# Three products of 12-bit parts in one Fourier stage, and a new order for two quarters, in a fused Fourier mixing and long-convolution kernel

## The chip, the core and the metric

The kernel runs on one core of one Trainium2 chip. The metric is the device time of one execution in microseconds (us); for a program on one core that is the time of that core. The core's engines work in parallel, each through its own list of instructions in fixed order: TensorE (PE, matmuls; PEld in the profile are its weight loads), VectorE (DVE), ScalarE (ACT), GpSimd (POOL) and SyncE (SP), which in this kernel issues nearly all DMA transfers. Engines wait for each other through semaphores. SBUF is the on-chip memory, PSUM the small memory that matmuls write to, in banks of 512 columns of 32-bit numbers.

## What is computed

Two heads that share nothing, put side by side. Head A is Fourier mixing of x (2048 x 512) by four given DFT matrices; head B is a long convolution of u with a kernel K that is made from state-space parameters.

```python
# A
a = einsum("bsd,ed->bse", x, dft_hid_re)
b = einsum("bsd,ed->bse", x, dft_hid_im)
y = einsum("ts,bse->bte", dft_seq_re, a) - einsum("ts,bse->bte", dft_seq_im, b)
# B
dt = exp(log_dt)
A = -exp(log_A_real) + 1j * A_imag
C = (C_real + 1j * C_imag) * dt[:, None]
P = exp((A * dt[:, None])[:, :, None] * pos[None, None, :])     # pos = 0..2047
K = 2.0 * einsum("dn,dnl->dl", C, P).real                       # 512 x 2048 taps
Kf, Uf = rfft(K, 4096), rfft(u.transpose(0, 2, 1), 4096)
y = irfft(Uf * Kf[None], 4096)[:, :, :2048].transpose(0, 2, 1) + u * D_skip
```

The results are 32-bit; inputs and outputs are too.

## The kernel before

**Head A (class `Fnet`), the stream.** All of A is 128 x 128 by 128 x 512 matmuls in 12 groups of four PSUM accumulators: eight groups over 16 tiles of x and the sequence matrices, whose results go to DRAM (`p`), then four groups over 8 tiles each of the hidden matrices and `p`. A 32-bit factor is cut in two parts, `hi` (a copy on ACT to the type `F32R`, which keeps 12 bits of the fraction, L184) and `lo` (the rest, a subtraction on DVE to the same type, L188). Each product is then three matmuls of one pass, hi·hi, hi·lo and lo·hi (L304): 1,920 in all. During the first group the raw tiles of x lie in a buffer named `uk` that is borrowed from head B (`loads`, L231) until all 16 are split.

**Head B (class `Ssm`).** The taps of K are sums of powers, made on DVE and ACT from tables (`tables1`, `tables2`, lines L543 to L684) in 16 chunks of 32 channels. For each chunk `taps` multiplies two tables on PE (L739, 128 small passes). Two chunks make one `stage1_k` (L769, eight in all): the first stage of the kernel's Fourier transform, its copies out of PSUM on ACT (L778) and a store to DRAM (`xk`, L783). `spectrum_u` and `stage1_u` do the same for u in eight calls: load (L808), four full-precision matmuls of 64 rows by 512 columns (L814; the chip runs each as two passes), copies on ACT (L824), store (`xu`, L830). The channels then go in four quarters h of 128, each in four groups q:

- `spectra` and `load_spectrum` load a group's part of `xu` and `xk` (L867), quarter by quarter, when all of that quarter's `xk` is stored (`xk_ev`);
- `products` and `product`: the second Fourier stage of u and k (L894, 64 passes), two copies on ACT (L906), six DVE operations for the complex product (L909 to L922), then the first stage of the inverse (`run`, L929, 32 passes), two copies on ACT (L944), a store to `zs` (L950);
- `inverses` and `inverse`: when all four groups of a quarter are stored, two loads from `zs` (L970), the last stage (L975, 32 passes), copies (L981) and the store of the result (L984).

The inverse's first stage has a way to join the taps: while taps are still to come (`taps_left`), a product hands its `run` to a list (`waiting`), and the next call of `taps` runs it right ahead of its own matmuls, in the same visit to PE and the same pair of PSUM slots. There are two such slots, of two banks each (`banks`, `give`), for all of head B.

**Buffers.** Head B has two sets of buffers. Set 0 has one buffer each of `xt`, `uk`, `z` and `zl` and is there from the start; set 1 has two of each and gets its memory only when the tables' memory is given back, after the last kernel's store (`tab_ev`). Quarters 0 to 2 use set 0, quarter 3 uses set 1 (`h // 3`).

**The order.** All instructions are put in order ahead of time, in Python, by a planner (class `Plan`). Each piece of work is a generator that names an engine and a duration before each instruction; the planner always takes the piece that can start first, and among equals the one of lower urgency number. It charges extra when PE changes between the stream and other work. The stream's matmuls have urgency 5, all other PE work less, so the stream fills what head B leaves. The stream's splits have urgency 0 (3 when three are ahead); u's stage has 1, tables 2 and more.

Of the kernel before, what the change touches and what calls it, by code (L numbers as in the profile page):

```python
# [365 lines left out]
class Ssm:  # L366


    def __init__(self, tc, ctx, plan, nd, ldt, dsk, uG, f1u, f1k, w2, ia, ib, out):
        self.tc, self.nc, self.plan = tc, tc.nc, plan  # L370
        self.nd, self.ldt, self.uG, self.out = nd, ldt, uG, out
        self.const = ctx.enter_context(tc.tile_pool(name="b_const", bufs=1))
        self.fps = ctx.enter_context(tc.tile_pool(name="b_fps", bufs=1, space=PSUM))
        dram = ctx.enter_context(tc.tile_pool(name="b_dram", bufs=1, space=DRAM))
        self.xu = dram.tile([64, 2, 32, DM], F32, name="xu")
        self.xk, self.zs = (dram.tile([4, 64, 2, 32, PART], F32, name=n) for n in ("xk", "zs"))
        self.dt_dram = dram.tile([128, 4], F32, name="dt_dram")
        self.par_dram = dram.tile([128, 4, DM - FIRST], F32, name="par_dram")
        first = ("f1u", f1u), ("f1k", f1k), ("dskip", dsk)
        second = ("w2", w2), ("ia", ia), ("ib", ib)  # L380
        self.cst = [[(n, self.const.tile([128, *a.shape[1:]], F32, name=n), a) for n, a in s] for s in (first, second)]
        self.halfpi = self.const.tile([128, 1], F32, name="halfpi")
        self.slots, self.fs, self.one = [0, 1], Sem(2), Sem(1)
        self.t1s, self.t2s, self.css = Sem(2), Sem(1), Sem(2)
        self.kss, self.res, self.xks = Sem(1), Sem(1), Sem(1)
        self.waiting, self.taps_left, self.pars = [], 16, Sem(1)
        self.sets, self.set_ev = {}, [Event(), Event()]
        self.const_ev, self.const2_ev, self.xu_ev = Event(), Event(), Event()
        self.xk_ev, self.zs_ev = [Event() for _ in range(4)], [Event() for _ in range(4)]

    def set_buffers(self, i, pool):
        self.sets[i] = Buffers(pool, i + 1)
# [12 lines left out]
    def constants(self, which, ev):  # L405
        yield "dma", sum(load(4 * math.prod(a.shape) / 1024) for _, _, a in self.cst[which])
        for n, t, a in self.cst[which]:
            self.nc.sync.dma_start(t, a)
            setattr(self, n, t)
        if ev is self.const_ev:  # L410
            yield "dve", 0.3
            self.nc.vector.tensor_scalar(self.dskip, self.dskip, 0.5, None, op0=OP.mult)
        self.plan.set(ev)

    def banks(self, n):

        yield self.one
        got = []
        for _ in range(n):
            yield self.fs  # L420
            k = self.slots.pop(0)
            got.append((k, self.fps.tile([128, 2, 512], F32, name=f"f{k}")))
        self.plan.put(self.one)
        return got

    def give(self, k):
        self.slots.append(k)
# [329 lines left out]
    def stage1_k(self, ks, n, ev):  # L757

        nc = self.nc
        yield ev  # L760
        yield "pool", 0.2
        nc.gpsimd.tensor_tensor(ks[:, :, 0], self.dskip[:, 16 * n:16 * n + 16], ks[:, :, 0], op=OP.add)
        yield self.const_ev
        got = yield from self.banks(2)
        yield "pe", 1.82
        for a in range(2):
            for j in range(4):
                r = slice(32 * j, 32 * j + 32)
                nc.tensor.matmul(got[j // 2][1][:, j % 2], self.f1k[r, a], ks[r, :, 32 * a:32 * a + 32],  # L769
                                 start=a == 0, stop=a == 1, tile_position=(32 * j, 0))  # L770
        self.plan.put(self.kss)
        yield self.xks
        xs = self.tab.tile([128, 32, 64], F32, name="xk_sb")
        for h, (k, p) in enumerate(got):
            for j in range(2):
                yield "act", act(512)
                o = 32 * h + 16 * j
                nc.scalar.activation(xs[:, :, o:o + 16], p[:, j].rearrange("p (i l) -> p l i", i=16), AF.Copy)  # L778
            self.give(k)
        xk = self.xk[n // 2].rearrange("s c l d -> (s c) l d")[:, :, 64 * (n % 2):64 * (n % 2) + 64]  # L780
        yield "dma", load(1024)
        for k in range(4):
            nc.sync.dma_start(xk[:, 8 * k:8 * k + 8], xs[:, 8 * k:8 * k + 8])  # L783
        self.plan.put(self.xks)
        if n % 2:
            self.plan.set(self.xk_ev[n // 2])
        if n == 7:
            self.plan.set(self.tab_ev)

    def spectrum_u(self):  # L790

        self.uleft = 16
        yield self.const_ev
        b = self.sets[0]
        yield b.zls
        self.xu_sb, self.xus = b.pool.tile([128, 2, 2, DM], F32, name="zl", bufs=b.n), Sem(2)
        for k in range(8):
            name = "uk"[k % 2]
            yield b.xts[name]
            if not k:  # L800
                self.u_sb = b.pool.tile([128, 2, 2, DM], F32, name="xt", bufs=b.n)
            self.plan.spawn(self.stage1_u(k, name), 1)

    def stage1_u(self, k, name):
        nc, b = self.nc, self.sets[0]
        u = self.u_sb[:, k % 2]
        yield "dma", load(512)
        nc.sync.dma_start(u, self.uG[:, 2 * k:2 * k + 2])  # L808
        got = yield from self.banks(2)
        yield "pe", 1.82  # L810
        for m in range(2):
            for r in range(2):
                rows = slice(64 * r, 64 * r + 64)
                nc.tensor.matmul(got[m][1][:, r], self.f1u[rows], u[rows, m], start=True, stop=True,  # L814
                                 tile_position=(64 * r, 0))
        self.plan.put(b.xts[name])
        for m in range(2):
            n = 2 * k + m
            sem = b.zbs if n % 3 == 2 else self.xus
            yield sem  # L820
            x = b.pool.tile([128, 2, DM], F32, name="z", bufs=b.n) if n % 3 == 2 else self.xu_sb[:, n % 3]
            for r in range(2):
                yield "act", act(512)
                nc.scalar.activation(x[:, r], got[m][1][:, r], AF.Copy)  # L824
            self.give(got[m][0])
            self.plan.spawn(self.store_u(x, 2 * k + m, sem), 1)

    def store_u(self, x, m, sem):
        yield "dma", load(512)
        self.nc.sync.dma_start(self.xu.rearrange("s c l d -> (s c) l d")[:, 2 * m:2 * m + 2], x)  # L830
        self.plan.put(sem)
        self.uleft -= 1
        if not self.uleft:
            self.plan.put(self.sets[0].zls)
            self.plan.set(self.xu_ev)

    def quarters(self):


        self.plan.spawn(self.constants(1, self.const2_ev), 3)  # L840
        self.left, self.xt = [4] * 4, {}
        self.xt_ev = {(n, h, q): Event() for n in "uk" for h in range(4) for q in range(4)}
        xu = [self.xu[:, :, :, PART * h:PART * h + PART] for h in range(4)]
        self.plan.spawn(self.spectra("u", xu, [self.xu_ev] * 4), 1)
        self.plan.spawn(self.spectra("k", [self.xk[h] for h in range(4)], self.xk_ev), 1)
        self.plan.spawn(self.products(), 1)
        for h in range(4):
            self.plan.spawn(self.inverses(h), 1)

    def spectra(self, name, x, evs):  # L850
        yield self.const2_ev
        for h in range(4):
            yield evs[h]
            yield self.set_ev[h // 3]
            b = self.sets[h // 3]
            view = x[h].rearrange("(q x g) c l d -> q (g c l) x d", q=8, x=4)
            for q in range(4):
                yield b.xts[name]
                self.plan.spawn(self.load_spectrum(b, name, h, q, view), 1)

    def load_spectrum(self, b, name, h, q, view):
        if (h, q) not in self.xt:
# [6 lines left out]

    def products(self):  # L870
        for h in range(4):
            yield self.set_ev[h // 3]
            b = self.sets[h // 3]
            for q in range(4):
                for n in "uk":
                    yield self.xt_ev[n, h, q]
                yield b.uks
# [5 lines left out]
    def product(self, b, h, q, got, done):  # L883
# [45 lines left out]
                        nc.tensor.matmul(got[xx // 2][1][64 * g:64 * g + 64, xx % 2, :2 * PART], self.ia[rows, c],  # L929
                                         Y[rows, :, g, 0], start=c == 0, stop=c == 1, tile_position=(32 * xx, 64 * g))  # L930
        w = Joined(self, run)
        if self.taps_left:
            self.waiting.append(w)
            yield w
        if w.got is None:
# [4 lines left out]
        yield b.zbs  # L940
        z = b.pool.tile([128, 2, 4, PART], F32, name="z", bufs=b.n)
        for n, (k, p) in enumerate(w.got):
            yield "act", act(512)
            a.activation(z[:, :, 2 * n:2 * n + 2].rearrange("p r x d -> p x r d"),  # L944
                         p[:, :, :2 * PART].rearrange("p x (r d) -> p x r d", r=2), AF.Copy)
            w.leave(k)
        view = self.zs[h].rearrange("(q x g) c l d -> q (g c l) x d", q=8, x=4)
        yield "dma", load(512)
# [114 lines left out]
```

## Time and profile before

| | us |
|---|---|
| three runs | 588.68, 590.52, 588.62 |
| median | 588.68 |
| the profiled execution | 590.22 |
| its span, first to last instruction | 588.4 |

| lines | what | instructions on PE |
|---|---|---|
| L304 | stream | 1,920 |
| L739 | taps | 2,048 |
| L769 | kernel, first Fourier stage | 128 |
| L814 | u, first Fourier stage | 64 |
| L894 | second Fourier stage | 1,024 |
| L929 | inverse, first stage | 512 |
| L975 | inverse, last stage | 256 |

How to read the profile: its second part cuts the span in 40 slices (14.7 us each here) and gives the busy share of each engine in tenths. PEclk is the granted clock of PE in tenths of full speed. A group's row has the line, the engine, the operation, output <- inputs by the program's names, the shapes and the count, then busy time, the mean ns of one, and the idle time of the engine just before, with what ended it. A matmul's recorded duration includes its way through the array and overlaps the next one, so the pace of matmuls is read from their starts. The chain of waits lists start, length and what ran, back from the last instruction. In the view of waits, a row has the total, the count and the longest wait. SPq and ACTq are the issues of transfers.

### The profile page before, as it was taken

Reading aid. Unit: us, or ns where it says so; the run is one execution under the profiler, and the core shown is the slowest. Engines: PE = TensorE matmul, PEld = TensorE weight load, DVE = VectorE, ACT = ScalarE, POOL = GpSimd, SP = SyncE. Lnnn points to the kernel's source line nnn. Section 1 sums busy time; section 2 is a strip of 40 time slices with the busy share of each in tenths; the row PEclk is TensorE's granted clock in tenths of the full one; section 3 lists DMA queues with packets and bytes.
Section 4 is the critical chain, followed back from the end, with each engine's and each line's share of the span. In section 5 each row is a group of like instructions: output and inputs, shape, how many; then the busy total and the mean of one; then the engine's idle time right before and its main releaser. Section 6 shows DMA issues by size and latency. Waiting matters only on the chain.

```text
span 588.4 us, 14902 instructions
## 1 busy us (share of the span) xinstructions
PE 580.2 (99%) x5958; PEld 439.7 (75%) x5958; DVE 496.5 (84%) x883; ACT 380.8 (65%) x745; POOL 4.7 (1%) x12
## 2 busy tenths in 40 slices
PE   8999999999999999999999999999999999999997
PEld 6767668778778777877687778777877776876785
DVE  7986989999999999999999999999999954245420
ACT  4789884946676677758674876577764635264622
POOL 0000000000000000000000000000000000000000
PEclk9999999999999999999999999999999999999999
DMA  8999996363493369446768684559798744998674
GB/s 262 329 367 338 337 342 199 101 188 81 122 280 106 89 170 264 137 135 165 246 183 259 168 246 128 136 158 284 225 282 234 230 131 148 283 354 263 190 251 144
DMA packets 141238, 125.84 MB, mean 214 GB/s; under 512 B 46192, under 2 KB 106352, under 8 KB 140912
## 3 DMA queue, kind: packets, MB, share of 16 engines
q1 hardware_dynamic: 140880, 124.48, 69.4%
q8 instruction: 47, 0.77, 0.5%
q10 hardware_dynamic: 288, 0.39, 0.2%
q14 instruction: 23, 0.19, 0.1%
HBM read 82.12 MB, written 42.73 MB: 212 GB/s over the span
## 4 chain that ended last, share of the span: by engine, by line
PE 69%; DVE 21%; issue 4%; DMA 3%; ACT 2%; SPq 1%; DVEq 0%; ACTq 0%
PE acc L304 52%; DVE prod L543 7%; DVE lo L188 4%; DVE t L552 4%; PE f L894 4%; PE f L739 3%; PE f L814 3%; PE f L975 3%; PE f L929 2%; PE f L769 2%; DMA xt<-xk 1%; DVE t L572 1%; DMA raw<-in_sT 1%; DVE t L566 1%; DVE cs L613 1%
## 5 line engine op out<-in xcount | busy, mean ns | idle before, releaser
L304 PE MATMUL acc<-hi,x_hi 128*128 128x512 f32 x640 | 257.2, 402 | 0.5 <-ACT x_hi L184 0.4
L304 PE MATMUL acc<-lo,x_hi 128*128 128x512 f32 x640 | 250.1, 391 | 1.5 <-issue 1.3
L304 PE MATMUL acc<-hi,x_lo 128*128 128x512 f32 x640 | 249.5, 390 | 0.1
L543 DVE TENSOR_TENSOR prod<-t,cs 128x1024 f32<-128x1024 f32 (+4 forms) x192 | 163.3, 869 | 3.6 <-ACT t L681 1.5
L188 DVE TENSOR_TENSOR lo<-raw,hi 128x512 fp32r<-128x512 f32 x160 | 109.1, 686 | 56.8 <-ACT hi L184 54.6
L304 PEld LDWEIGHTS acc<-hi,x_hi 128*128 128x128 f32 x640 | 120.1, 188 | 49.2 <-issue 21.2
L184 ACT ACTIVATE hi<-raw 128x512 fp32r<-128x512 f32 x160 | 100.1, 628 | 85.8 <-PE acc L304 64.7
L304 PEld LDWEIGHTS acc<-hi,x_lo 128*128 128x128 f32 x640 | 120.2, 188 | 28.0 <-issue 1.5
L304 PEld LDWEIGHTS acc<-lo,x_hi 128*128 128x128 f32 x640 | 120.2, 188 | 23.8 <-DVE lo L188 0.9
L552 DVE TENSOR_TENSOR t<-prod 128x512 f32<-128x512 f32 (+4 forms) x192 | 94.3, 510 | 1.1
L559 ACT ACTIVATE square<-t 128x256 f32<-128x256 f32 (+1 forms) x64 | 36.6, 572 | 24.6 <-DVE t L552 22.5
L327 ACT ACTIVATE y<-acc 128x512 f32<-128x512 f32 x47 | 27.9, 598 | 12.8 <-PE acc L304 9.5
L906 ACT ACTIVATE uk<-f 128x1024 f32<-128x1024 f32 x32 | 32.1, 1017 | 4.8 <-PE f L894 4.8
L739 PEld LDWEIGHTS f<-t,t 128*32 128x32 f32 x2048 | 29.4, 110 | 6.8 <-issue 4.1
L739 PE MATMUL f<-t,t 128*32 128x64 f32 x2048 | 32.2, 220 | 0.6 <-issue 0.6
L894 PE MATMUL f<-xt,w 64*32 64x256 f32 x1024 | 31.3, 379 | 0.0
L909 DVE TENSOR_TENSOR z<-uk 128x512 f32<-128x512 f32 x32 | 21.9, 685 | 8.3 <-ACT uk L906 4.7
L894 PEld LDWEIGHTS f<-xt,w 64*32 64x32 f32 x1024 | 18.4, 106 | 10.9 <-issue 4.6
L944 ACT ACTIVATE z<-f 128x512 f32<-128x512 f32 x32 | 17.6, 596 | 11.8 <-PE f L739 6.4
L572 DVE TENSOR_TENSOR t<-square 128x128 f32<-128x128 f32 (+1 forms) x64 | 24.6, 385 | 0.3 <-ACT square L559 0.3
L618 ACT ACTIVATE cs<-cs 128x352 f32<-128x352 f32 x32 | 15.9, 536 | 12.2 <-DVE cs L613 12.2
L911 DVE TENSOR_TENSOR uk<-uk 128x512 f32<-128x512 f32 x32 | 22.1, 690 | 0.8
(81 smaller groups left out, 409.7 us busy)
## 6 DMA issues: line engine op xcount, KB each, us to landing
raw<-in_sT SPq DMA_DIRECT2D x127, 256.0 KB, 3.3
p<-y SPq DMA_DIRECT2D x32, 256.0 KB, 4.1
xt<-xu SPq DMA_DIRECT2D x32, 256.0 KB, 4.4
xk<-xk_sb SPq DMA_DIRECT2D x32, 256.0 KB, 4.0
xt<-xk SPq DMA_DIRECT2D x32, 256.0 KB, 5.0
zs<-z SPq DMA_DIRECT2D x32, 256.0 KB, 3.4
zl<-zs SPq DMA_DIRECT2D x16, 512.0 KB, 5.9
raw<-p SPq DMA_DIRECT2D x32, 256.0 KB, 3.8
```

Source lines behind the costliest of these rows:

```text
L184: self.nc.scalar.activation(hi, src, AF.Copy)
L188: self.nc.vector.tensor_tensor(lo, src, hi.bitcast(F32), op=OP.subtract)
L304: nc.tensor.matmul(acc[d], l[:, cols], r, start=k == 0 and n == 0, stop=k == len(items) - 1 and n == 2)
L327: self.nc.scalar.activation(y, ps, AF.Copy, scale=-1.0 if g[2] == 1 else 1.0)
L543: self.nc.vector.tensor_tensor(p.rearrange("p k d c m -> p k (d c) m"), src.rearrange("p d c l -> p (d c) l")[:, None, :, rows].to_broadca ...
L552: self.nc.vector.tensor_tensor(dst[:, :, :, rows], p[:, 0], p[:, 1, :, ::-1], op=OP.add)
L559: self.nc.scalar.activation(sq, t[:, :, :, m // 2:m], AF.Square)
L572: self.nc.vector.tensor_tensor(t[:, :, 0, m:2 * m:2], box[0][:, :, 0], box[0][:, :, 1], op=OP.subtract)
L739: nc.tensor.matmul(ps[32 * j:32 * j + 32, i], t1[:, d, c], t2[:, d, c], start=c == 0, stop=c == 1, tile_position=(0, 32 * j))
L894: nc.tensor.matmul(both[:, :, c], self.w2[rows, 2 * q + r, xx, 32 * c:32 * c + 32], xt[rows, r, xx], start=True, stop=True, tile_position= ...
L906: a.activation(uk[:, r].rearrange("p g n c d -> p g (n c d)"), p, AF.Copy)
L911: v.tensor_tensor(t[:, r], t[:, r], u[:, r, :, ::-1], op=OP.mult)
```

## The change

The change has three parts.

1. **u's first stage in three products.** The constant `f1u` is cut in `f1u_hi` and `f1u_lo` once, and each of u's eight loads (1024 columns) in `hi` and `lo`, by one ACT copy and one DVE subtraction. The matmuls become three of one pass for each of the four before: 12 passes in place of 8. The two halves lie in set 0's `uk` buffer (`u_hl`, one pair, guarded by `u_free`), so the stage begins only when the raw x have left it, and the buffer is held until the last store of `xu`.
2. **The third quarter's inverses without taps.** Only quarters 0 and 1 hand their `run` to the taps (`h < 2`); later ones take PSUM slots of their own.
3. **The last quarter's first group in the first buffers.** `place` gives group 0 of quarter 3 to set 0, the others to set 1. Events of `xk` are kept for each group; the last kernel store (n = 7) is cut by rows into four stores (`store_k`), one for each group, in place of four by columns. In the last `stage1_k` every second copy out of PSUM goes to DVE, and in quarter 3 the second of the two copies L944 too (`copy`).

```diff
@@ constants
+            self.f1u_hi = self.const.tile([128, 128], F32R, name="f1u_hi")
+            yield "act", act(128)
+            self.nc.scalar.activation(self.f1u_hi, self.f1u, AF.Copy)
+            yield "dve", dve(128)
+            self.f1u_lo = self.const.tile([128, 128], F32R, name="f1u_lo")
+            self.nc.vector.tensor_tensor(self.f1u_lo, self.f1u, self.f1u_hi.bitcast(F32), op=OP.subtract)
@@ new
+    def copy(self, to, src, vector):
+        if vector:
+            yield "dve", dve(512)
+            self.nc.vector.tensor_copy(to, src)
+        else:
+            yield "act", act(512)
+            self.nc.scalar.activation(to, src, AF.Copy)
@@ stage1_k
-                nc.scalar.activation(xs[:, :, o:o + 16], p[:, j].rearrange("p (i l) -> p l i", i=16), AF.Copy)
+                yield from self.copy(xs[:, :, o:o + 16], p[:, j].rearrange("p (i l) -> p l i", i=16), n == 7 and j)
...
-        yield "dma", load(1024)
-        for k in range(4):
-            nc.sync.dma_start(xk[:, 8 * k:8 * k + 8], xs[:, 8 * k:8 * k + 8])
+        if n < 7:
+            yield "dma", load(1024)
+            for k in range(4):
+                nc.sync.dma_start(xk[:, 8 * k:8 * k + 8], xs[:, 8 * k:8 * k + 8])
+        else:
+            for k in range(4):
+                self.plan.spawn(self.store_k(xk, xs, k), 1)
+            yield self.xk_ev[3][3]
...
+    def store_k(self, xk, xs, q):
+        yield "dma", load(256)
+        self.nc.sync.dma_start(xk[32 * q:32 * q + 32], xs[32 * q:32 * q + 32])
+        self.plan.set(self.xk_ev[3][q])
@@ spectrum_u
+        yield b.uks
+        self.u_hl, self.u_free = b.pool.tile([128, 2, 2, DM], F32R, name="uk", bufs=b.n), Sem(1)
@@ stage1_u
+        yield self.u_free
+        hi, lo = self.u_hl[:, 0], self.u_hl[:, 1]
+        yield "act", act(1024)
+        nc.scalar.activation(hi, u, AF.Copy)
+        yield "dve", dve(1024)
+        nc.vector.tensor_tensor(lo, u, hi.bitcast(F32), op=OP.subtract)
         got = yield from self.banks(2)
-        yield "pe", 1.82
+        yield "pe", 1.42
+        f_hi, f_lo = self.f1u_hi, self.f1u_lo
         for m in range(2):
-            for r in range(2):
-                rows = slice(64 * r, 64 * r + 64)
-                nc.tensor.matmul(got[m][1][:, r], self.f1u[rows], u[rows, m], start=True, stop=True,
-                                 tile_position=(64 * r, 0))
+            for n, (f, v) in enumerate(((f_hi, hi), (f_hi, lo), (f_lo, hi))):
+                for r in range(2):
+                    rows = slice(64 * r, 64 * r + 64)
+                    nc.tensor.matmul(got[m][1][:, r], f[rows], v[rows, m], start=n == 0, stop=n == 2,
+                                     tile_position=(64 * r, 0))
+        self.plan.put(self.u_free)
@@ store_u (after the last store)
+            self.plan.put(self.sets[0].uks)
@@ spectra
-            yield evs[h]
-            yield self.set_ev[h // 3]
-            b = self.sets[h // 3]
...
             for q in range(4):
+                yield evs[h][q]
+                yield self.set_ev[self.place(h, q)]
+                b = self.sets[self.place(h, q)]
                 yield b.xts[name]
                 self.plan.spawn(self.load_spectrum(b, name, h, q, view), 1)
+
+    def place(self, h, q):
+        return int(h == 3 and q > 0)
@@ products: the same choice of the set, for each group
@@ product
-        if self.taps_left:
+        if self.taps_left and h < 2:
             self.waiting.append(w)
             yield w
...
-            yield "act", act(512)
-            a.activation(z[:, :, 2 * n:2 * n + 2].rearrange("p r x d -> p x r d"),
-                         p[:, :, :2 * PART].rearrange("p x (r d) -> p x r d", r=2), AF.Copy)
+            yield from self.copy(z[:, :, 2 * n:2 * n + 2].rearrange("p r x d -> p x r d"),
+                                 p[:, :, :2 * PART].rearrange("p x (r d) -> p x r d", r=2), h == 3 and n)
```

More of the change, by code (lines that the diff above doesn't have):

```diff
@@ L388, in __init__ @@
         self.const_ev, self.const2_ev, self.xu_ev = Event(), Event(), Event()
-        self.xk_ev, self.zs_ev = [Event() for _ in range(4)], [Event() for _ in range(4)]
+        self.xk_ev, self.zs_ev = [[Event() for _ in range(4)] for _ in range(4)], [Event() for _ in range(4)]
     def set_buffers(self, i, pool):
@@ L775, in stage1_k @@
             for j in range(2):
-                yield "act", act(512)
                 o = 32 * h + 16 * j
-                nc.scalar.activation(xs[:, :, o:o + 16], p[:, j].rearrange("p (i l) -> p l i", i=16), AF.Copy)
+                yield from self.copy(xs[:, :, o:o + 16], p[:, j].rearrange("p (i l) -> p l i", i=16), n == 7 and j)
             self.give(k)
         xk = self.xk[n // 2].rearrange("s c l d -> (s c) l d")[:, :, 64 * (n % 2):64 * (n % 2) + 64]
-        yield "dma", load(1024)
-        for k in range(4):
-            nc.sync.dma_start(xk[:, 8 * k:8 * k + 8], xs[:, 8 * k:8 * k + 8])
+        if n < 7:
[6 more added lines that the diff above has]
+            yield self.xk_ev[3][3]
         self.plan.put(self.xks)
-        if n % 2:
-            self.plan.set(self.xk_ev[n // 2])
+        if n % 2 and n < 7:
+            for ev in self.xk_ev[n // 2]:
+                self.plan.set(ev)
         if n == 7:
             self.plan.set(self.tab_ev)
+    def store_k(self, xk, xs, q):
+        yield "dma", load(256)
+        self.nc.sync.dma_start(xk[32 * q:32 * q + 32], xs[32 * q:32 * q + 32])
+        self.plan.set(self.xk_ev[3][q])
     def spectrum_u(self):
@@ L871, in products @@
         for h in range(4):
-            yield self.set_ev[h // 3]
-            b = self.sets[h // 3]
             for q in range(4):
+                yield self.set_ev[self.place(h, q)]
+                b = self.sets[self.place(h, q)]
                 for n in "uk":
```

3 lines of the change are left out of this document (1 added, 2 removed).

## The prediction, made before the changed kernel ran

> **What bounds the kernel now.** I began with the page's busy times and slices, then went to the waits of TensorE (PE), the order of its runs in the chain of waits, and the busy time by stretches.
>
> ```profile
> span 588.4 us, 14902 instructions
> ...
> PE 580.2 (99%) x5958; PEld 439.7 (75%) x5958; DVE 496.5 (84%) x883; ACT 380.8 (65%) x745; POOL 4.7 (1%) x12
> ...
> DVE  7986989999999999999999999999999954245420
> PEclk9999999999999999999999999999999999999999
> ```
>
> PE is busy 99% of the span at full granted clock, and VectorE (DVE) is full up to slice 32 (of 14.7 us each, so to about 478 us) and nearly idle after it. A busy PE can still be stretched by waiting, so the next view is what PE waited for, in all:
>
> ```profile
> PE acc L204 <- DVE y L201: 1.6, 1, 1.6
> PE acc L304 <- issue: 1.3, 1, 1.3
> PE f L739 <- issue: 0.6, 1, 0.6
> PE acc L304 <- ACT x_hi L184: 0.4, 1, 0.4
> PE acc L304 <- ACT y L327: 0.2, 1, 0.2
> PE acc L304 <- DVE lo L188: 0.2, 1, 0.2
> ```
>
> These are 4.3 us in 588.4. The Fourier mixing's matmuls (L304, the stream) are there to fill every hole that the convolution leaves. So the end is the sum of PE's work, and an edit is worth what it takes off that sum, as long as the stream can fill and the convolution does not become the last to finish. The unit prices, from the timeline (first and last of 36 stream matmuls in a row) and from the chain:
>
> ```profile
> 469.64 0.39 PE L304 MATMUL acc<-hi,x_hi 128*128 128x512 f32 x1
> ...
> 477.57 0.39 PE L304 MATMUL acc<-hi,x_lo 128*128 128x512 f32 x1
> ```
>
> ```profile
> 27.78 1.92 PE f L814 x8
> 29.69 5.66 PE acc L304 x24
> ...
> 329.77 1.93 PE f L769 x16
> ...
> 423.25 1.05 PE f L929 x32
> 424.30 1.93 PE f L739 x128
> ...
> 453.31 1.05 PE f L929 x32
> ...
> 477.96 1.05 PE f L929 x32
> ...
> 483.90 1.89 PE f L894 x64
> ...
> 492.18 1.93 PE f L769 x16
> ...
> 499.10 1.05 PE f L929 x32
> ...
> 521.57 2.00 PE f L975 x32
> ...
> 538.89 1.90 PE f L975 x32
> ...
> 576.32 1.90 PE f L975 x32
> 578.22 6.36 PE acc L304 x27
> ```
>
> A stream matmul (12-bit parts, 512 columns) takes 7.93 / 35 = 0.2266 us. 24 of them between two runs of the convolution take 5.66 us, 0.22 more than 24 x 0.2266 = 5.44: that is the price of leaving the stream and coming back. One run of u's first stage (L814) is eight passes, two for each of four full-precision matmuls, and takes 1.92 us: 8 x 0.2266 = 1.81 and 0.11 at the ends. Two passes work at a time, one in each half of the rows, so one full-precision pass lasts 2 x 0.2266 us.
>
> **The change part by part.**
>
> *u's first stage, PE.* Each of its eight runs has twelve single passes where it had eight. No row of the trace has such a pass in half the rows. The low bound is that the two halves work side by side, as the full-precision passes do: 6 x 0.2266 + 0.11 = 1.47 us. The high bound is that the halves take turns: 12 x 0.2266 + 0.11 = 2.83 us. I take 1.47, because every resource that such a pair needs is already seen in use at that pace: L769 runs four row groups at once, 16 passes in 1.93 us, so one pass of 512 columns, with its output and its weight load, each 0.12 us, against 12 in 1.36 us or 0.113 us here; and the pace of one bank's output, 512 columns in 0.2266 us, is that of the stream. So each run saves 1.92 - 1.47 = 0.45 us, and eight save **3.6 us**; at the high bound eight cost 7.3 us more. The break-even is a run of 1.92 us, a pair in 0.30 us.
>
> The weight loads need a closer look:
>
> ```profile
> L304 PEld LDWEIGHTS acc<-hi,x_hi 128*128 128x128 f32 x640 | 120.1, 188 | 49.2 <-issue 21.2
> L814 PEld LDWEIGHTS f<-xt,f1u 64*128 64x128 f32 x64 | 5.5, 186 | 6.6 <-issue 5.5 <-ACT zl L824 0.4 <-ACT cs L618 0.2
> ```
>
> A load is recorded with 0.19 us, and the stream has one for each matmul, in the same rows, at a pace of 0.2266 us: it is hidden behind the matmul before it. Two loads in the time of one pair would be 0.37 us if they followed each other, but L769's come every 0.12 us with the same 128 columns, so they overlap. [...]
>
> *u's first stage, ACT and DVE.* Each run now needs one copy of 1024 columns on ScalarE (ACT) and one subtraction of 1024 on DVE, and the constants need one of 128 columns on each. The nearest rows:
>
> ```profile
> L906 ACT ACTIVATE uk<-f 128x1024 f32<-128x1024 f32 x32 | 32.1, 1017 | 4.8 <-PE f L894 4.8
> ...
> L224 DVE TENSOR_TENSOR x_lo<-uk,x_hi 128x128 fp32r<-128x128 f32 x1 | 0.3, 291 | 2.4 <-ACT x_hi L222 2.4
> ```
>
> ```profile
> L543 DVE TENSOR_TENSOR prod<-t,cs 128x1024 f32<-128x1024 f32 x96 | 117.1, 1219 | 1.1
> ```
>
> ```profile
> 28.00:83.00 55.00, 55.00 (x239) 36.22 (x239) 47.11 (x85) 50.15 (x105) 0.00 (x0) 1.00 0.98 345
> 83.00:478.00 395.00, 392.65 (x4515) 303.59 (x4523) 387.98 (x688) 265.93 (x535) 4.24 (x7) 1.00 0.64 186
> ```
>
> (The columns of the last fence are length, then busy time of PE, weight loads, DVE, ACT and POOL, granted clock, DMA share, GB/s.) ACT gets 8 x 1.02 = 8.1 us, DVE 8 x 1.22 + 0.29 = 10.0 us. The stage has 7.9 us of idle DVE and 4.9 us of idle ACT between 28 and 83 us. The halves live in the `uk` buffer, which holds the raw x until the last x is split:
>
> ```profile
> 39.12 0.69 DVE L188 TENSOR_TENSOR x_lo<-uk,x_hi 128x512 fp32r<-128x512 f32 x1 [0.28 <-ACT x_hi L184]
> ```
>
> ```profile
> 164.09 0.93 SPq L867 DMA_DIRECT2D xt<-xk  x2
> ```
>
> So the stage starts later, around 40 us, and ends around 100; x's loads run ahead of it without u's beside them, where DMA is 98% busy now. The first product waits for its kernel part, loaded at 164.09, so u's spectrum stays early enough. On PE all this costs nothing while the stream covers it; its splits go first on both engines (urgency 0 against 1). If that cover is gone, ACT's rest, 8.1 - 4.9 = 3.2 us, falls on PE (third rival). What is late next is the tables: DVE is full from 83 to 478 us (388 of 395), so the tables end between 10.0 - 7.9 = 2 and 10 us later. I take 5.
>
> *Third quarter without taps.* Three of its four inverses are now joined to taps (423.25, 453.31 and 477.96, each with a run of L739 behind it), the fourth at 499.10 is alone already. Alone, each leaves the stream and comes back by itself: 3 x 0.22 = **0.7 us** more on PE; at best, next to another run by chance, 0. In return the quarter no longer paces itself by the taps. It also brings the fourth group's six DVE operations (4.1 us at 0.69) ahead of the tables' end, so I count the last table up to 9 us later.
>
> *Last quarter.* Its first group uses the first set's buffers, so its u part can be loaded before the tables' memory is free, and its k part waits for one quarter of the store instead of all four. The four stores carry the same bytes; SP has the same number of issues, with u's two earlier. Half of the last copies out of PSUM go to DVE, which is nearly idle there. None of this touches the sum on PE; it only sets how long the convolution's last stage takes, as does the next view:
>
> ```profile
> 481.00 0.60 ACT L749 ACTIVATE ks<-f 128x512 f32<-128x512 f32 x1 [3.00 <-PE f L739]
> ...
> 488.12 0.63 ACT L184 ACTIVATE hi<-raw 128x512 fp32r<-128x512 f32 x1 [4.24 <-PE acc L304]
> ...
> 490.04 1.03 ACT L906 ACTIVATE uk<-f 128x1024 f32<-128x1024 f32 x1
> ...
> 585.52 0.36 ACTq L324 DMA_DIRECT2D out_ya<-y  x1
> ```
>
> ```profile
> 575.90 3.87 SPq L984 DMA_DIRECT2D out_yb<-zl  x2
> ```
>
> The last taps' copy is done at 481.6, but the last kernel's stage (L769) runs only at 492.18: both PSUM slots are held by the third quarter's fourth product (483.90), whose copies on ACT stand behind a stream split that waits 4.24 us, until 491.1. With that product gone early, these 10 us take up the 9 us of delay. The two inverses of the third quarter at 521.57 and 538.89 leave the last stage too. The convolution's last issue ends at 579.8, the stream's stands at 585.5: 5.7 us of slack, 2.8 us after the saving. So I expect the stream to stay last.
>
> *Sum.* -3.6 + 0.7 = -2.9 us on the path. The profiled execution took 590.22 us, its span and 1.8 us around it, and would take 587.3; it stands 1.5 us above the median of the runs, 588.68, which becomes **585.8 us**.
>
> **The rivals.**
> 1. *The two halves take turns* (slower). Place: the eight runs of u's first stage; price 8 x (2.83 - 1.92) + 0.7 = +8.0 us, so 596.7; it decides from a pair longer than 0.30 us. For it: no row shows such passes in half the rows. Against it: L814 and L769 show two and four row groups at the same pace for one group's pass (1.92 us for 8, 1.93 for 16). 5 in 100. [...]
> 2. *Weight loads show.* A pair costs 0.2266 + 0.19 us, a run 2.6 us: +5.5 + 0.7, so 594.9. For it: loads of 0.19 us and twice as many for the time; against it: the paces above. 4 in 100.
> 3. *The early stage gives the saving back.* ACT is busy 50.15 of 55 us there already; stream splits or u's halves come late behind a queue in fixed order, and PE stands 3.2 us: 585.8 + 3.2 = 589.0, no change. For it: ACT's load, and the 4.24 us wait shown above, which is of this kind. Against it: in those 55 us PE now has no idle time at all. 14 in 100.
> 4. *The convolution's end takes over.* If the last stage gets no shorter and the tables end 10 us later, its last issue comes 10.0 - 2.8 = 7.2 us behind the stream's: 593.0. For it: a full DVE from 83 to 478 us; against it: the 10 us of held slots and the inverses that leave. 7 in 100.
>
> **How the numbers follow.** The forecast gets 70 in 100, 585.8 us with its own range 584 to 587.3: 0.2 us a run for the ends and order, and 1.5 us for stalls that come or go. A measurement of this kernel tells a difference from about 0.3% (1.8 us), so faster means under 586.9. From the forecast 64 and from the third rival 2 in 100 are faster; same: 6 and 11; slower: the first, second and fourth rivals (16) and 1 of the third. The range 583.3 to 591 holds the forecast and the third rival, and leaves out the 16 and a few on the low side.
>
> **What would show it.** Right: runs of u's first stage of 12 passes in about 1.47 us, starting near 40 us; third-quarter inverses (L929) with the stream on both sides, done before 478; PE waits still about 4 us; stream matmuls as the last work, some 3 us earlier, and the convolution's last store well ahead of them. Wrong: runs of 2 us or more (rivals 1, 2); PE waits of 3 us or more between 28 and 110 us (3); inverses (L975) as PE's last run, with idle time before them (4).

## The result, and the profile after

The changed kernel took 597.03 us (median of 6 runs, 594.94 to 599.38), the kernel before 589.75 us in the same comparison (588.62 to 592.38): a ratio of 1.0124, 95% interval 1.009 to 1.0158. It is slower by 1.2%, where I had forecast 0.5% faster. The time is the one that the first rival had priced (596.7), but the profile shows that it is not that rival's doing.

First the page of the changed kernel, and its view of what PE waited for (total, count, longest):

```profile
span 595.0 us, 14993 instructions
...
PE 579.2 (97%) x5990; PEld 442.6 (74%) x5990; DVE 508.1 (85%) x898; ACT 387.1 (65%) x748; POOL 4.8 (1%) x12
...
DVE  7999999999999999999998969998999993265420
```

```profile
PE f L754 <- issue: 5.4, 3, 2.1
PE f L935 <- DMA xt<-xk: 2.0, 1, 2.0
PE acc L204 <- DVE y L201: 1.6, 1, 1.6
PE acc L304 <- ACT y L327: 1.5, 2, 0.9
PE f L935 <- issue: 0.7, 1, 0.7
PE f L754 <- ACT uk L947: 0.5, 1, 0.5
PE acc L304 <- DVE lo L188: 0.3, 1, 0.3
```

PE is busy for less time than before (579.2 against 580.2 us) in a span that is 6.6 us longer. It waits 12.0 us where it waited 4.3. The largest row has 5.4 us inside the taps' runs (L754, which was L739 and had 0.6), put down to "issue", that is, to nothing that the profile shows. The chain of waits has the runs themselves:

```profile
55.57 1.59 PE f L849 x12
57.16 7.70 PE acc L304 x33
...
130.63 1.59 PE f L849 x12
...
431.09 1.05 PE f L970 x32
432.14 2.27 PE acc L304 x9
...
521.66 4.68 DMA xt<-xk
526.34 1.96 PE f L935 x64
...
580.27 1.90 PE f L1015 x32
582.17 9.08 PE acc L304 x39
```

u's first stage (L849) takes 1.59 us a run, less than the 1.92 us before: the two halves of the rows do work side by side. The stage starts at 55.6 us, not at 40, and ends at 132, not around 100. The third quarter's inverses (L970, which was L929) stand alone, the last of them at 491.6 us, not before 478. The stream is still the last work on PE. The timeline of PE around the three stops:

```profile
316.05 0.31 PE L754 MATMUL f<-t,t 128*32 128x64 f32 x5 [1.63 <-issue]
...
351.91 0.24 PE L754 MATMUL f<-t,t 128*32 128x64 f32 x1 [2.09 <-issue]
...
408.48 0.42 PE L754 MATMUL f<-t,t 128*32 128x64 f32 x13 [1.67 <-issue]
```

Each stop cuts one run of taps in two, near its end: 5, 1 and 13 matmuls of 128 are left over. Measured from start to start, against a normal pace of 15 ns, the stops cost 1.83, 2.29 and 1.87 us, 6.0 us together. The kernel before had two such stops, of 1.48 and 0.77 us (its rows of 1.3 and 0.6 us of "issue").

From the starts on PE, the end of its last matmul, 584.56 us before and 591.24 us after, is made up like this:

| | us |
|---|---|
| u's first stage, 8 x (1.59 - 1.92) | -2.6 |
| three more visits of the stream | +0.7 |
| stops for "issue", 6.0 against 2.2 | +3.7 |
| waits at the last quarter's first two products (L935), 0.74 and 2.12 | +2.9 |
| other waits, 3.1 against 1.8, of which 1.04 near 52 us and 0.81 near 168 us are new | +1.3 |
| not assigned | +0.7 |
| sum | +6.7 |

### The profile page after: what moved, and what is told of

The parts are those of the page before. It is cut to its first block, busy times and chain, and to the rows that moved or that the text cites. A ratio compares the mean times of both kernels' runs of the same rounds, so it can differ in the third digit from the quotient of the medians.

```text
span 595.0 us, 14993 instructions
## 1 busy us (share of the span) xinstructions
PE 579.2 (97%) x5990; PEld 442.6 (74%) x5990; DVE 508.1 (85%) x898; ACT 387.1 (65%) x748; POOL 4.8 (1%) x12
## 4 chain that ended last, share of the span: by engine, by line
PE 85%; DVE 4%; ACT 3%; DMA 3%; issue 3%; SPq 1%; DVEq 0%; ACTq 0%
PE acc L304 65%; PE f L754 5%; PE f L935 4%; PE f L970 3%; PE f L784 3%; PE f L1015 2%; PE f L849 2%; DVE lo L188 1%; DMA p<-y 1%; DMA out_yb<-zl 1%; ACT hi L184 1%; DMA xt<-xk 1%; DMA cs<-in_ldt 1%; ACT y L327 1%; DVE x_lo L188 1%
## 5 line engine op out<-in xcount | busy, mean ns | idle before, releaser
L558 DVE TENSOR_TENSOR prod<-t,cs 128x1024 f32<-128x1024 f32 (+3 forms) x192 | 164.1, 870 | 9.9 <-ACT t L696 8.1
L327 ACT ACTIVATE y<-acc 128x512 f32<-128x512 f32 x47 | 27.9, 595 | 17.1 <-PE acc L304 14.4
L754 PEld LDWEIGHTS f<-t,t 128*32 128x32 f32 x2048 | 29.7, 110 | 12.3 <-issue 7.7
L754 PE MATMUL f<-t,t 128*32 128x64 f32 x2048 | 32.7, 220 | 5.9 <-issue 5.4
L935 PE MATMUL f<-xt,w 64*32 64x256 f32 x1024 | 31.5, 379 | 2.7 <-DMA xt<-xk 2.0
L935 PEld LDWEIGHTS f<-xt,w 64*32 64x32 f32 x1024 | 18.6, 106 | 13.7 <-issue 7.4
L439 ACT ACTIVATE z<-f 128x512 f32<-128x512 f32 x28 | 15.7, 597 | 18.2 <-PE f L970 10.1
L581 DVE SCALAR_TENSOR_TENSOR t<-t 128x128 f32<-128x128 f32 (+2 forms) x48 | 22.3, 465 | 0.3
```

The source lines that it names most:

```text
L327: self.nc.scalar.activation(y, ps, AF.Copy, scale=-1.0 if g[2] == 1 else 1.0)
L558: self.nc.vector.tensor_tensor(p.rearrange("p k d c m -> p k (d c) m"), src.rearrange("p d c l -> p (d c) l")[:, None, :, rows].to_broadca ...
L581: self.nc.vector.scalar_tensor_tensor(t[:, :, 1, m:2 * m:2], t[:, :, 0, m // 2:m], 2.0, t[:, :, 1, m // 2:m], op0=OP.mult, op1=OP.mult)
L754: nc.tensor.matmul(ps[32 * j:32 * j + 32, i], t1[:, d, c], t2[:, d, c], start=c == 0, stop=c == 1, tile_position=(0, 32 * j))
L935: nc.tensor.matmul(both[:, :, c], self.w2[rows, 2 * q + r, xx, 32 * c:32 * c + 32], xt[rows, r, xx], start=True, stop=True, tile_position= ...
```

## The experiments

**What the stops have in common.** The page's list of queues names one that carries instructions:

```profile
q8 instruction: 47, 0.77, 0.5%
```

47 transfers of 16,384 bytes. PE has 12,072 recorded instructions, 257 for each transfer. My estimate from these two numbers is one transfer, a block, for every 256 instructions of PE's list. The starts bear it out: when the nth transfer begins, PE has started 153 to 449 instructions more than 256 x (n - 1), all through the kernel, so the queue keeps step with PE's list. The starts and lengths of these transfers stand in the trace, and three of them meet the three stops (us):

```
transfer 313.4 to 314.5    stop until 316.05
transfer 349.6 to 350.5    stop until 351.91
transfer 406.0 to 407.0    stop until 408.48
```

Counted from 0 over all of PE's recorded instructions, the stops stand after number 6,080, 6,848 and 8,128: all 192 more than a multiple of 256. The two of the kernel before stand after 5,312 and 7,360, again 192 more than a multiple. So theory A: PE uses up a block before the next one is there. An inverse and the taps joined behind it are 64 and 256 instructions in 3.0 us; a border that falls near their end leaves PE less time than the 2.63, 2.30 and 2.52 us that passed here from the start of a transfer to the end of its stop. The trace agrees: from the start of a transfer to the moment when PE has used up all instructions up to the next border it is 0, 0.63 and 0.78 us at the three stops, and 3.7 us or more at every other border. To test the theory, the borders can be moved without touching the order of anything, by small matmuls in the warm-up, which works on zeros. From the starts in a trace one can then work out which borders will fall badly.

**1. The borders moved by 72.** Two of the three wide warm-up matmuls are replaced by 20 small ones (the trace has 40 passes for the 20, each with its load, so a full-precision matmul is four instructions).

```diff
-        for n in range(3):
-            self.nc.tensor.matmul(ps[:, :256], z[:, :128], z[:, 256:], start=n == 0, stop=n == 2)
+        for n in range(1):
+            self.nc.tensor.matmul(ps[:, :256], z[:, :128], z[:, 256:], start=n == 0, stop=n == 0)
+        for n in range(20):
+            self.nc.tensor.matmul(ps[:8, 256:264], z[:, :8], z[:, 256:264], start=n == 0, stop=n == 19)
```

> The changed kernel with 72 more small instructions on PE in the warm-up (20 matmuls of 8 columns in place of two of 256); every other instruction and its order is as it was. Theory A: the three stops of about 2 us inside the taps' runs (L754 at 314, 350 and 407 us of the changed kernel, 6.0 us together) are PE out of instructions: its list comes in blocks of 256 instructions (16 KB), and a block that is used up in a dense stretch of taps is gone before the next is there. Moving the block borders by 72 instructions takes all three away; total 4 to 6 us below the changed kernel, 591 to 593. Rival B: the stops belong to these places in the order (a wait that the profile does not name); they stay, and the time is 597 give or take 1, or about 0.5 us later for the longer warm-up.

590.14 us, ratio to before 1.0003 (0.9986 to 1.002): 7 us less for 72 tiny instructions, a little more than the 4 to 6 us expected. What PE waited for in this kernel:

```profile
PE acc L204 <- DVE y L201: 1.6, 1, 1.6
PE acc L306 <- ACT y L329: 1.5, 2, 0.9
PE f L937 <- DMA xt<-xk: 0.9, 1, 0.9
PE acc L306 <- ACT hi L184: 0.7, 1, 0.7
```

No row of "issue" is left, and the wait for the last quarter's k part has fallen from 2.9 to 0.9 us as well. Rival B, a wait that belongs to the place in the order, is out: the order is the same.

**2. The last store by columns.** The changed kernel with the last kernel store cut as in the others, so that the last quarter's loads wait for all of it.

```diff
-        if n < 7:
+        if True:
...
-        if n % 2 and n < 7:
+        if n % 2:
```

> The changed kernel with the last kernel store cut by columns again (four stores of all 128 partitions), the loads of the last quarter waiting for all four. Theory C: the four stores by rows of 32 partitions are slow (7 to 8 us each against 4), so the last quarter's first k parts come late and PE stands 2.9 us at L935 near 515 and 524 us; with columns the stores land in about 4 us, the two waits go, total 2 to 3 us below the changed kernel, 594 to 595. Rival D: the stores are slow because of what else moves at that moment, and the waits come from the number of loads queued behind them; landing stays above 6 us and the time stays at 597 give or take 1.

597.38 us, ratio 1.0114 (1.0089 to 1.0138): no change in time that can be told from the changed kernel's. The two waits at L935 are gone, and PE's last matmul ends 1.5 us earlier (589.69), but the runs do not show it; the three stops are there (5.9 us). The stores by columns took 6.9 to 7.6 us for the first three, by rows 8.2 to 7.0. So it is not the shape that makes the landing slow: theory C falls there, and what rival D says of landing and time came out. But D explains the waits by the loads queued behind the stores, and the waits went although the stores landed as slowly: what decides them was not shown. In the changed kernel's own order on SP, one of the stores stands behind loads of the stream that wait for a buffer:

```profile
502.43 0.65 SPq L812 DMA_DIRECT2D xk<-xk_sb  x1
504.77 0.33 SPq L272 DMA_DIRECT2D raw<-p  x1
505.14 4.59 SPq L812 DMA_DIRECT2D xk<-xk_sb  x2
509.83 1.82 SPq L272 DMA_DIRECT2D raw<-p  x1
511.70 0.56 SPq L812 DMA_DIRECT2D xk<-xk_sb  x1
```

**3. The kernel before, made worse.** 168 more instructions; again nothing else.

```diff
+        for n in range(44):
+            self.nc.tensor.matmul(ps[:8, 256:264], z[:, :8], z[:, 256:264], start=n == 0, stop=n == 43)
```

> The kernel before with 168 more small instructions on PE in the warm-up, nothing else. Theory A: the borders of the blocks of 256 now fall so that three to four of the taps' runs empty a block too early (worked out from the starts in the trace of before); stops inside L739 add up to 4 to 7 us instead of 2.2, and the time rises by 2 to 5 us above before (plus up to 1.5 us for the longer warm-up, seen apart in the first 6 us of the profile). Rival B: the stops stay at 286 and 371 us, and the time rises by the warm-up alone.

593.63 us, ratio 1.0056 (1.0035 to 1.0078). Three stops near 259, 341 and 429 us, 4.4 us together, as expected, and none where they were. In the profile PE's last matmul ends 6.0 us later than before: 2.2 us are stops, 2.2 us a colder start, which is told with the ninth experiment, and the rest are new waits for DMA in the last quarter. So the kernel before can be made 3 us slower by instructions that do nothing, but only part of that is the borders.

**4. The first part alone.** The kernel before with u's first stage in three products (the diff shown for `constants`, `spectrum_u`, `stage1_u` and `store_u`), its planner run anew.

> The kernel before with u's first stage in three products, the other two parts of the change left out. The order is planned anew. Theory: the stage itself is worth 8 x (1.92 - 1.59) = 2.6 us on PE, and what the changed kernel lost besides is stops for instructions and waits at the last quarter, not the stage: work on PE falls by 2.6 us; the time is before minus 2.6 us plus or minus the change in stops inside the taps' runs (0 to 4 us), so 586 to 591. Rival E: the stage's copies and subtractions in the full early part delay the stream and the tables; waits of PE before 110 us add 3 us or more over before's, and the time is 592 or more.

597.2 us, ratio 1.0115 (1.0096 to 1.0134): the range 586 to 591 was missed. Rival E has the time right but not the cause: between 10 and 110 us PE waits 1.4 us, not 3. The three stops stand at the same three numbers as in the changed kernel (6.5 us), and the new waits near 52 and 168 us are there with the same sizes, 1.04 and 0.81 us. So the first part brings both, and the other two parts do not. This profile also shows what a stop can set off. Its timeline of PE, and its busy time by stretches (length; PE, weight loads, DVE, ACT, POOL; granted clock; DMA share; GB/s):

```profile
352.76 0.24 PE L745 MATMUL f<-t,t 128*32 128x64 f32 x1 [2.09 <-issue]
352.94 0.67 PE L304 MATMUL acc<-hi,x_hi 128*128 128x512 f32 x1
353.41 0.63 PE L304 MATMUL acc<-lo,x_hi 128*128 128x512 f32 x1
353.83 0.63 PE L304 MATMUL acc<-hi,x_lo 128*128 128x512 f32 x1
```

```profile
350.00:353.00 3.00, 0.91 (x51) 0.68 (x40) 0.42 (x1) 0.00 (x0) 0.00 (x0) 1.00 1.06 341
353.00:357.00 4.00, 4.00 (x12) 3.14 (x12) 1.89 (x6) 2.23 (x7) 0.00 (x0) 0.57 0.53 151
```

After a stop of 2.3 us (2.1 us of idle time) the granted clock is 0.5 for 3.4 us, and stream matmuls start 0.43 us apart, not 0.23: some 1.7 us more. It did not fall after three stops of 1.8 to 2.3 us in the changed kernel's profile, nor after one of 2.6 us in the second experiment's, so length alone does not decide; the last section comes back to it. The end of the first part alone is the convolution's (issues on SP):

```profile
591.26 0.33 SPq L321 DMA_DIRECT2D out_ya<-y  x1
591.93 0.38 SPq L1002 DMA_DIRECT2D out_yb<-zl  x1
```

**5. The control to the first.** The same kind of warm-up, with as many instructions as in the changed kernel (the edit is against the first experiment).

```diff
-        for n in range(20):
+        for n in range(2):
```

> Control to the shift: the changed kernel with the warm-up of the first experiment's kind (one wide and two small matmuls) but with the same number of instructions as in the changed kernel, so the borders of the blocks stay where they were. Theory A: the three stops inside the taps' runs are back at about 314, 350 and 407 us, 5 to 7 us together, and the time is 597 give or take 1.5. Rival F: it was the shorter wide part of the warm-up that helped; then the stops stay away and the time is near 590.

599.63 us, ratio 1.0136 (1.01 to 1.0171), above the expected 597 give or take 1.5. The stops are back, after the same numbers 6,080, 6,848 and 8,128 (4.2 us together, less than expected). A wait of 2.4 us for the last quarter came with them, and the granted clock fell to half for 3.4 us after it; the colder start took 1.9 us. The shift did it, not the kind of warm-up.

**6. The kernel before, made better.** A shift of 136, for which the starts gave no stop.

> The kernel before with 136 more small instructions on PE in the warm-up. Theory A: worked out from the starts in the trace of before, no block is emptied too early with this shift; its two stops (1.5 us at 286, 0.8 us at 371) go and nothing takes their place; PE's last matmul ends 1.5 to 2.3 us earlier, after up to 0.5 us for the longer warm-up; time 0.2 to 0.4% under before. Rival B: time as before or up to 0.5 us more.

Both stops went and none came: no row of "issue" is left among its waits. But the time is 590.6 us, ratio 0.9988 (0.997 to 1.0006), which is no difference that can be told from before, and PE's last matmul ends at 584.89 us, 0.3 us later than before. The colder start took 1.9 us, not the 0.5 that I had allowed (the stream's 96th matmul starts at 29.24 us, in before at 27.39), and three new waits of 0.3 to 0.5 us the rest.

**7. The first part alone, borders moved by 72.**

> u's first stage in three products alone, as in the fourth experiment, with 72 more small instructions in the warm-up. The three stops of 6.5 us go. If the stream then ends last, the time is 597.2 - 6.5 = 590.7 or lower, and the other two parts of the change are worth nothing; if the convolution's last stage ends last, its store is the last transfer to land, PE has idle time before the last inverses (L993), and the time lies 1 us or more above that of the changed kernel with the same shift (590.1).

592.36 us, ratio 1.0016 (1.0001 to 1.0032). The three stops are gone; one of 1.3 us near 432 us has come, again 192 past a multiple of 256. The convolution's store is the last to be issued (586.82 us, the stream's last two at 586.15 and 586.62), and the kernel is 2.2 us above the whole change with the same shift in the medians, 0.13% or 0.8 us in the ratios to before, whose intervals overlap, so the times alone do not tell the two apart. The profiles show what the second and third part do: without them the span ends 5.5 us after PE's last matmul, and the convolution's store lands last, at 590.3 us, 1.4 us behind the stream's; in the first experiment the span ends 3.8 us after it, and a store of the stream lands last. My fourth rival is what happens without them.

**8. The second and third part alone.** The changed kernel with `stage1_u` and its neighbours as before.

> The changed kernel with u's first stage as it was before, so the second and third part of the change alone. Work on PE: 0.7 us more than before for the three inverses that go by themselves. The rest is where the borders of the blocks fall in the new order: before had 2.2 us of stops, so the time is before - 2.2 + 0.7 + its own stops, 589 plus 0 to 6 us. The convolution's last inverse ends 8 us or more ahead of the kernel's end, where it was 10 us in before; waits of PE before 110 us are those of before (under 1.5 us), if those of the changed kernel come from u's copies.

592.97 us, ratio 1.0025 (1.001 to 1.0041). Its stops are before's two, a little longer, and one of 0.65 us at 88 us; 3.5 us in all. At the last quarter's products (L917) PE waits another 1.3 us. The convolution's last inverse ends 18.6 us ahead of PE's last matmul. The waits near 52 and 168 us are not there: they come from the first part. In the changed kernel the timeline of ACT shows the one near 52 us:

```profile
51.64 1.04 ACT L839 ACTIVATE uk<-xt 128x1024 fp32r<-128x1024 f32 x1
52.59 0.58 ACT L327 ACTIVATE y<-acc 128x512 f32<-128x512 f32 x1
```

The stream's copy out of PSUM (L327) stands behind u's copy of 1.0 us, and PE waits for the accumulator.

**9 and 10. Both kernels without stops and with a warm start.** The first experiment paid for its small warm-up: its 96th stream matmul starts at 29.01 us against 27.36 in the changed kernel, because the first dozen start 0.43 us apart; the granted clock is 1.0 only from 10.1 us on, in the changed kernel from 6.4. Here the extra instructions stream about as many columns as the wide warm-up did.

```diff
+        for n in range(21):
+            self.nc.tensor.matmul(ps[:32, :36], z[:, :32], z[:, 256:292], start=n == 0, stop=n == 20)
```

> The changed kernel with 72 more instructions in the warm-up again, but now 21 matmuls of 36 columns that stream about as many columns as the three of 256. In the first experiment PE began at half pace (the stream's 96th matmul at 29.0 us, 27.4 in the changed kernel), 1.6 us for the small warm-up. If the clock follows the columns streamed, the 96th matmul is back at 27.4 to 27.8, no stops in the taps' runs, and the time is 1.2 to 1.6 us under the first experiment, 588.5 to 589, 0.3% under before. If it needs full-size weights or something else, the 96th stays at 29 us and the time at 590.

589.68 us, ratio 0.9979 (0.9966 to 0.9993): the changed kernel, with 72 instructions more, is 0.2% faster than the kernel before. The start is back (27.51 us). Against the first experiment 0.5 us was won in the medians and 1.4 us in the ratios to before, but the profile does not show it: PE's last matmul ends 0.5 us later there, since PE now waits near 36 us too (1.24 and 0.58 us for the stream's splits). Three of its waits:

```profile
PE acc L304 <- ACT y L327: 1.5, 2, 0.9
PE acc L304 <- ACT hi L184: 1.3, 2, 1.1
PE f L935 <- DMA xt<-xk: 1.2, 1, 1.2
```

> The kernel before with 136 more instructions in a warm-up of 37 matmuls of 20 columns. The shift of 136 took before's two stops away, and the cold start gave 1.9 us back. With the stream's 96th matmul at 27.4 to 27.9 the time is 1.5 to 2.2 us under before, 588.3 to 589.3; then the change itself is worth 0.2% or less, either way, once neither kernel stops for instructions. If the changed kernel with the shift is more than 1.5 us faster than this one, the change keeps most of its 2 us of work after all.

590.51 us, ratio 0.9999 (0.9985 to 1.0012). Here the warm-up came out 1.2 us too long (the stream begins at 5.64 us, the 96th matmul at 28.64), so the expected gain did not show. Its PE has no stop and no wait over 0.2 us after the start:

```profile
PE acc L204 <- DVE y L201: 1.6, 1, 1.6
PE acc L304 <- DVE lo L188: 0.2, 1, 0.2
PE acc L304 <- ACT y L327: 0.2, 1, 0.2
```

Its PE ends at 583.66 us; the changed kernel's of the ninth experiment ends at 584.06, although its stream begins 1.1 us earlier. In the times the changed kernel is 0.8 us ahead in the medians and 1.2 in the ratios, about what the late start cost the other. So free of stops the two are level, as far as these runs can tell: what u's stage saves on PE is paid back in waits for ACT and for the last k part, some 4 us more of them than here.


## Why the prediction was wrong

**The step that failed** is the condition under which the sum was made: "an edit is worth what it takes off that sum, as long as the stream can fill and the convolution does not become the last to finish". The stream did not fill the stops, in which PE, by theory A, had no instructions. The 1.3 and 0.6 us of "issue" in the waits of before were quoted and read as a small constant, and the forecast left 1.5 us for "stalls that come or go". They were the price of where two block borders fell. The changed kernel has 32 more matmuls and their loads in u's stage and another order, so all later borders fell elsewhere: 6.0 us of stops instead of 2.2. Taking them away took 7 us off the time (experiment 1), more than their 6.0 us, although the colder start cost 1.6; the wait for the last quarter's k part fell by 1.9 us with them. Stops are the largest of four misses: on PE the forecast was -2.9 us and the profile has +6.7, and of these 9.6 us the stops are 3.7, the last quarter's first products 2.9, other new waits 1.3 and the size of u's stage 1.0; 0.7 is not assigned.

**u's first stage on PE** was right in kind and too large: 1.59 us a run, not 1.47, so 2.6 us and not 3.6. The two passes of a pair start 3 to 17 ns apart, and behind the first pair they follow every 0.23 us, as forecast; the ends of a run cost 0.23 us, not 0.11. That was mis-sized in before already: behind the first its passes follow every 0.43 us, not 2 x 0.2266 = 0.453, and its ends were 0.20 us.

**The first two rivals** (halves in turn; weight loads showing) are out: a pair takes 0.23 us. The serial price does not appear, and no run shows a load of 0.19 us added to the 0.2266 us of a pair, as the second rival's sum has it. That the first rival's time was met is chance.

**The third rival** was half right: u's copies do hold up the stream, 1.04 and 0.81 us near 52 and 168 us, and only where the first part is in the kernel. It was priced at 3.2 us, with its sign between 28 and 110 us, where the changed kernel waits 1.5.

**The fourth rival** did not decide: in the changed kernel the last inverse ends on PE 9 us before the stream. Without parts two and three it does decide, by some 2 us (experiments 4 and 7: the span ends 5.9 and 5.5 us after PE's last matmul, in the changed kernel 3.8). The reading of the last quarter was right on that: the last kernel's stage now follows the last taps by 2.2 us, where it was 11.2, and the third quarter's two last stages come 13 and 7 us earlier. The tables themselves were further off: the last taps end 15.3 us later than before (496.2 against 480.9), where I counted up to 9; in the first experiment, without the stops, they end 9.8 us later.

**Where an edit was costed at nothing**: the four stores of the last kernel. They stand on SP between stream loads that wait for DVE, the first two products' k part came late, and PE stood 2.9 us in front of L935. In the changed kernel without stops it was 0.9 to 1.3 us (experiments 1 and 9). That the order on SP is the cause is read from the trace; no run shows it.

**The third quarter alone** cost its three visits (65 runs of the stream against 62), 0.7 us as forecast.

## What to carry to other kernels

Where an engine runs close to full, look at the waits that the profile puts down to "issue" and count which instruction they stand at. Here those inside the runs of taps and of the stream were all 192 above a multiple of 256, a shift of 72 instructions took the changed kernel's three stops (6.0 us) away, and so the time of each edit contained a draw of where the borders fell. Compare two orders only after such stops are taken out of both, for instance by shifting the borders with a few instructions at the start, and look at what these cost there. And a forecast that adds up the work of a full engine must leave room for stops of this size in a stretch like the taps', whose matmuls start 15 ns apart.

## What was not expected of the hardware

All 21 stops that stand inside a run of taps or of the stream and have "issue" to their name (0.65 to 2.6 us each, in eight profiles of five different orders) come after an instruction of PE whose number is 192 above a multiple of 256. All of them end 1.2 to 1.6 us after the transfer of a block of 16,384 bytes has ended, 2.2 to 2.9 us after it began. In all twelve profiles a border costs a stop where PE reaches it 1.8 us or less after the transfer began, and none where it is 2.15 us or more. They come inside a run of taps or up to 3.3 us behind it; elsewhere the same transfers cost nothing.

The granted clock fell to 0.5 for 3.4 us after an idle time of 2.1 us in the fourth experiment's profile and of 2.4 us in the fifth's. It did not fall after 2.1 us in the changed kernel's profile, nor after 2.4 us in the second experiment's. What decides it was not shown: two falls are few, and no run was made to test it.

A warm-up of many tiny matmuls did not bring PE to its full pace. With the first experiment's warm-up the first dozen stream matmuls start 0.43 us apart. With one wide matmul and 2 to 44 of 8 columns (experiments 1, 3, 5, 6 and 7) the granted clock reached 1.0 at 10.1 to 10.7 us, with the wide warm-up at 4.8 to 6.4, with 37 matmuls of 20 columns at 8.5 and with 21 of 36 columns at 4.9.
